# A row maximum that takes the factor as its scale, one bound operation for two heads, and bucket numbers turned by a small matmul, in hashed attention with a gated feed-forward behind it

## Chip, cores and metric

The kernel runs on one NeuronCore of a Trainium2 chip. The metric is device microseconds of one execution, from the first to the last instruction and what the runtime adds around it. Three runs of the kernel before gave 927.25, 927.81 and 928.17 us; the median is 927.81 us. The profile is of one more execution, of 924.44 us, in which the span of the instructions is 922.7 us.

## What is computed

The reference is attention in which a query sees only the keys of its own bucket, and then a feed-forward layer whose two inner products are multiplied with each other:

```python
q_bits = (np.einsum('bhsd,dk->bhsk', q, proj) > 0)      # batch 4, 8 heads, 768 rows, width 64; 6 bits
k_bits = (np.einsum('bhsd,dk->bhsk', k, proj) > 0)
mask = q_bucket[:, :, :, None] == k_bucket[:, :, None, :]   # bucket: the 6 bits as a number
scores = np.where(mask, q @ k.T / np.sqrt(64), -1e9)
attn = np.exp(scores - scores.max(-1)); attn /= attn.sum(-1) + 1e-09
x = (attn @ v), heads side by side                      # 3072 tokens x 512
out = ((x @ w_a) * (x @ w_b)) @ w_out                   # 512 -> 1536 -> 512
```

A query whose bucket holds no key gets equal weights, since all its scores are -1e9. Inputs and output are float32; the kernel splits nearly every operand into a high and a low float16 part and adds three matmul products for one.

## The kernel before

**Attention.** The 3072 tokens are taken in chunks of 128 or 256 (14 chunks; the first five are batch 0). Batch 0 has a path of its own (bits appended to the operands as extra rows, `qtile`). In batches 1 to 3 the work goes by pairs: 128 queries of two heads (72 pairs, so 144 tiles of 128 queries by 768 keys). A pair runs so:

- TensorE: 12 matmuls of the scores `s` for both heads into two PSUM buffers, of which there are only two (tag "s", L1286).
- VectorE: for each head the mask `hp` (L1333): -2^60 where the key's bucket number, held in all partitions as `trk[:, 1]`, differs from the query's. Then one custom operation (L1342) that writes e = scores + mask and the row maximum `mx`.
- VectorE: `bound`, two small operations for each head: `sc` (L1350), the factor cq = 1/8 times the scales of the q and k splits, or 0 where no key matched; and `bias` (L1354), 14 ln 2 - mx * sc, for which the constant `lnv` is held as a tile.
- ScalarE: exp(sc * e + bias) with the row sum (L1362).
- Split of e into two float16 parts `a`: the high part by ScalarE, VectorE or GpSimd (`cast`, L555), the low part by GpSimd or VectorE (`minus`, L558). A DMA transposes both into `at`, and 18 matmuls with v make `av` (L1263).

**Bucket numbers of the keys.** `split_pairs` makes, for each of the 12 head pairs of batches 1 to 3, a [128, 12] tile `bkk` of bucket numbers (row = key position within a block). They go to DRAM by one DMA, `buckets` (L852), come back broadcast to all partitions over the no longer needed raw keys `rk` (L857), and a copy on ScalarE or GpSimd (L555, out `trk`) puts them into the order by head and block.

**Feed-forward.** For each chunk `moe` issues 24 groups of `ab` matmuls (L1572; L1564 for the first two chunks, whose operands stay float32) into three PSUM buffers, ScalarE scales one product (`a`, L1593), VectorE multiplies it with the other (`g`, L1601), ScalarE and GpSimd split that into two float16 parts (L1612, L1617), and `o` matmuls (L1637) add them up. `osb` takes the result out.

**Order.** Every operation is recorded with `op`, and issued in the order of the table `ORDER`; `ENGINE_OF` says for operations that may run on two engines which one does. Each engine then runs its instructions in just that order, and waits at the head of its queue for what the next one needs. DMAs are issued from SyncE's queue, in order too.

Of the kernel before, what the change touches and what calls it, by code (L numbers as in the profile page):

```python
# [1747 lines left out]
```

## Time and profile before

| | |
|---|---|
| runs | 927.25, 927.81, 928.17 us |
| profiled execution | 924.44 us, span 922.7 us |
| TensorE matmul | 869.7 us busy (94%) |
| VectorE | 754.5 us (82%), 1839 instructions |
| ScalarE | 584.8 us (63%) |
| GpSimd | 380.9 us (41%) |
| TensorE's granted clock | full but for two short stretches, 0.996 in the mean |

The program is one long overlap: attention of later chunks beside the feed-forward of earlier ones. It begins with loads and the splitting of the first operands, and ends with some 90 us in which only the last feed-forward chunks are left. Matmul rows are pipelined and their ends are modelled, so TensorE's busy time also covers part of its short waits. An engine's waiting time is listed with the instruction that waited and with what ended the wait.

### The profile page before, as it was taken

What the parts mean: (1) busy time and instruction counts of PE and PEld (TensorE: products, weight loads), DVE (VectorE), ACT (ScalarE), POOL (GpSimd) and SP (SyncE); (2) the same over time, 40 slices, a digit from 0 to 9 for tenths busy, and PEclk for the clock granted to TensorE, in tenths of its full rate; (3) what the DMA queues carried; (4) which work ended last, traced back from release to release, by engine and by line L of the source; (5) the groups of instructions that cost most, each with busy time, mean ns of one, the idle gap of its engine ahead of it and who ended that gap; (6) DMA issues with size and microseconds to landing.
All of it is one profiled execution on the core that took longest, in us unless ns stands there. A gap on an engine that the chain in (4) does not pass through costs nothing. (4 is left out here: it accounts for less than half of the span.)

```text
span 922.7 us, 25179 instructions
## 1 busy us (share of the span) xinstructions
PE 869.7 (94%) x10049; PEld 653.4 (71%) x10049; DVE 754.5 (82%) x1839; ACT 584.8 (63%) x1130; POOL 380.9 (41%) x348
## 2 busy tenths in 40 slices
PE   5899999999999999999989999998999999999997
PEld 4788777677776666777666776766666777777775
DVE  7998999988879989868998889889879889974211
ACT  6878667566877677767556676565685665554222
POOL 1445546456465443442444442324433444432111
PEclk9999999999999999999999999999999999999999
DMA  9979997789889978988777877788877857776300
GB/s 328 299 246 262 163 166 147 127 162 194 162 166 163 178 133 138 162 172 181 147 150 121 133 139 126 143 161 159 151 152 146 140 113 125 116 126 98 48 35 24
DMA packets 396070, 140.69 MB, mean 152 GB/s; under 512 B 368176, under 2 KB 386736, under 8 KB 395952
## 3 DMA queue, kind: packets, MB, share of 16 engines
q1 hardware_dynamic: 395792, 139.08, 77.9%
q8 instruction: 78, 1.28, 0.6%
q14 instruction: 40, 0.33, 0.1%
q10 hardware_dynamic: 160, 0.00, 0.0%
HBM read 42.54 MB, written 6.33 MB: 53 GB/s over the span
## 5 line engine op out<-in xcount | busy, mean ns | idle before, releaser
L1572 PE MATMUL ab<-xT,wz 128*128 128x256 f16 (+1 forms) x3456 | 377.8, 264 | 14.3 <-DVE g L1601 9.7
L1572 PEld LDWEIGHTS <-wz 128*128 128x128 f16 x3456 | 308.6, 98 | 67.0 <-issue 26.4
L558 POOL TENSOR_TENSOR a<-e,a 128x768 f16<-128x768 f32 x123 | 207.6, 1691 | 141.5 <-ACT a L555 81.6
L1617 POOL TENSOR_TENSOR g<-g,g 128x256 f16<-128x256 f32 x132 | 96.9, 734 | 301.9 <-ACT g L1612 285.6
L1637 PE MATMUL o<-wz,g 128*128 128x512 f16 (+1 forms) x840 | 215.4, 392 | 1.2 <-DVE g L1601 0.6
L1362 ACT ACTIVATE e<-e,bias,sc 128x768 f32<-128x768 f32 x144 | 147.3, 1023 | 65.0 <-DVE bias L1354 64.7
L1342 DVE CUSTOM_DVE_ANT_0 e<-s,hp 128x768 f32<-128x768 f32 x144 | 136.1, 950 | 11.9 <-PE s L1286 7.3
L1263 PEld LDWEIGHTS <-at 128*128 128x128 f16 x3312 | 114.5, 98 | 31.9 <-DMA at<-a 12.3
L1593 ACT ACTIVATE a<-ab,ab 128x256 f32<-128x256 f32 x132 | 61.9, 469 | 115.6 <-PE ab L1572 109.6
L1601 DVE SCALAR_TENSOR_TENSOR g<-ab,ab,a 128x256 f32<-128x256 f32 x132 | 63.3, 479 | 83.7 <-ACT a L1593 71.3
L1263 PE MATMUL av<-vh,at 128*128 128x64 f16 x2208 | 121.0, 193 | 7.3 <-DMA at<-a 6.4
L1637 PEld LDWEIGHTS <-g 128*128 128x128 f16 x792 | 72.7, 98 | 72.3 <-issue 4.3
L1612 ACT CAST g<-g 128x256 f16<-128x256 f32 x132 | 52.9, 400 | 66.6 <-DVE g L1601 53.2
L555 ACT CAST a<-e 128x768 f16<-128x768 f32 x110 | 90.8, 827 | 5.1 <-DMA at<-a 3.0
L1286 PE MATMUL s<-trk,trq 64*128 64x384 f16 x864 | 86.5, 324 | 3.6 <-DVE mx L1342 2.9
L1354 DVE SCALAR_TENSOR_TENSOR bias<-mx,sc,lnv 128x1 f32<-128x1 f32 x144 | 73.2, 509 | 5.1
L1333 DVE TENSOR_SCALAR hp<-trk,bkq 128x768 bf16<-128x768 f16 x144 | 68.9, 492 | 3.0 <-ACT trk L555 2.0
L1286 PEld LDWEIGHTS <-trq 64*128 64x128 f16 x864 | 38.6, 94 | 39.0 <-issue 17.8
L558 DVE TENSOR_TENSOR a<-e,a 128x768 f16<-128x768 f32 x61 | 59.5, 977 | 5.9 <-ACT a L555 5.4
L1392 ACT ACTIVATE e<-s,bias,sc 128x768 f32<-128x768 f32 x48 | 47.4, 988 | 24.7 <-DVE bias L1383 13.5
L1263 PE MATMUL av<-vl,at 128*128 128x64 f16 x1104 | 62.4, 193 | 0.0
L1371 DVE TENSOR_REDUCE mx<-s 128x1 f32<-128x768 f32 x48 | 45.6, 950 | 4.8 <-PE s L1309 4.8
(206 smaller groups left out, 1063.7 us busy)
## 6 DMA issues: line engine op xcount, KB each, us to landing
rq<-in_q_dram SPq DMA_DIRECT2D x24, 256.0 KB, 3.7
rk<-in_k_dram SPq DMA_DIRECT2D x16, 384.0 KB, 4.3
wz<-in_moe_w_a_dram SPq DMA_DIRECT2D x12, 512.0 KB, 6.4
wz<-in_moe_w_b_dram SPq DMA_DIRECT2D x12, 512.0 KB, 5.0
...
```

Source lines behind the costliest of these rows:

```text
L555: {"ACT": nc.scalar.copy, "DVE": nc.vector.tensor_copy, "POOL": nc.gpsimd.tensor_copy}[e](out=out, in_=x)
L558: (nc.gpsimd if e == "POOL" else nc.vector).tensor_tensor(out=out, in0=x, in1=y, op=ALU.subtract)
L1263: nc.tensor.matmul(av.t[:, u, :], lhsT=at.t[:, a + kt, :], rhs=w.t[:, h, kt, :], start=i == 0, stop=i == 3 * NT - 1,)
L1286: nc.tensor.matmul(ps[h].t[:, jj, :HALF], lhsT=trq.t[rows, 0, qp * nq + j * nt + t], rhs=tr.t[rows, 0, k0 : k0 + NT // 2].rearrange("p n s ...
L1333: lambda: nc.vector.tensor_scalar(out=apart(), in0=tr.t[:, 1, h * NT : (h + 1) * NT].rearrange("p n s -> p (n s)"), scalar1=qbk[m, half].t ...
L1342: lambda: nc.vector.tensor_tensor_reduce(out=flat2(e.t), in0=halves(ps.t), in1=flat2(apart()), scale=1.0, scalar=-3.0e38, op0=ALU.add, op1 ...
L1354: nc.vector.scalar_tensor_tensor(out=bias.t[:, col], in0=mx.t[:, col], scalar=sc.t[:, col], in1=lnv, op0=ALU.mult, op1=ALU.subtract, rever ...
L1362: lambda: nc.scalar.activation(e.t, e.t, AF.Exp, bias=bias.t[:, col], scale=sc.t[:, col], accum_out=sm.t[:, u : u + 1]),
L1572: nc.tensor.matmul(pl.t[:, m, to], lhsT=wt(m, wi, cc, f), rhs=xt.t[:, cc * nt // NC, xi, cc * nt % NC : cc * nt % NC + nt, :], start=i == ...
L1601: lambda a=a, g32=g32, pl=pl, gr=gr, sc_of=sc_of: nc.vector.scalar_tensor_tensor(out=g32.t, in0=pl.t[:, 1, :CH], scalar=sc_of(gr + 1), in1 ...
L1617: lambda g=g, g32=g32, g_of=g_of: nc.gpsimd.tensor_tensor(out=g_of(g[1]), in0=g32.t, in1=g_of(g[0]), op=ALU.subtract),
L1637: nc.tensor.matmul(po[u].t.rearrange("p a b -> p (a b)"), lhsT=x()[:, us], rhs=w, start=f == 0 and i == 0, stop=f == NF - 1 and i == len(t ...
```

## The change

1. The custom maximum takes the factor cq as its `scale` operand in place of 1.0, so e = cq * scores + mask and `mx` is already scaled. `sc` goes; exp has no scale operand; a row in which no key matches keeps -2^60 in e and in `mx`, and the bias cancels it.
2. `bound` is one operation for both heads of a pair, [128, 2]: bias = 14 ln 2 - mx, and may run on VectorE or GpSimd. Both maxima come before it, and both exps after it. `lnv` goes.
3. The key buckets, now bfloat16, are turned by a matmul with the identity into PSUM (`kn`, 12 x 128), copied to SBUF by ScalarE or VectorE, written to DRAM as 12 rows of 256 bytes, and read back broadcast straight into `trk[:, 1]`. The copy out of `rk` goes. The blocks now lie as (block, head), so the mask reads every second block of 128.
4. `ORDER` and `ENGINE_OF` are new. Operations were renumbered; the engines' queues are the same up to about the first ninth of TensorE's.

```diff
-        line = nc.dram_tensor(f"buckets_{x}", [P, n], F16, kind="Internal").ap()
-        op(
-            "SP", DMA_ISSUE, lambda: nc.sync.dma_start(out=line, in_=bk.t), key, r=[bk], w=[("line", x)], svc=0.1,
-        )
-        over = lambda: raw.t.bitcast(F16)
+        pst = psum(f"{which}n_{x}", tag)
+        op("PE", 0.08, lambda: nc.tensor.matmul(pst.t[:n, 0, :P], lhsT=bk.t, rhs=identb, start=True, stop=True),
+           key, r=[bk, "identb"], w=[pst])
+        turned_bk = lambda: bits.t.bitcast(BF16)[:n, :P]
+        op(
+            "ACT DVE", {"ACT": 0.2, "DVE": 0.2}, lambda e: cast(e, turned_bk(), pst.t[:n, 0, :P]), key, r=[pst, bk],
+            w=[(bits, 2)],
+        )
+        line = nc.dram_tensor(f"buckets_{x}", [n, P], BF16, kind="Internal").ap()
+        op(
+            "SP", DMA_ISSUE, lambda: nc.sync.dma_start(out=line, in_=turned_bk()), key, r=[(bits, 2)],
+            w=[("line", x)], svc=0.1,
+        )
         op(
             "SP", DMA_ISSUE,
             lambda: nc.sync.dma_start(
-                out=over(), in_=line.rearrange("p n -> (p n)").unsqueeze(0).to_broadcast([P, P * n])
+                out=dst.t[:, 1].rearrange("p n s -> p (n s)").bitcast(BF16),
+                in_=line.rearrange("n p -> (n p)").unsqueeze(0).to_broadcast([P, P * n]),
             ),
-            key, r=[("line", x)], w=[raw], svc=1.3,
-        )
-        op(
-            "ACT POOL", {"ACT": 1.5, "POOL": 1.65},
-            lambda e: cast(
-                e, dst.t[:, 1].rearrange("p (h t) s -> p h t s", h=2), over().rearrange("p (s t h) -> p h t s", t=nb, h=2)
-            ),
-            key, r=[raw], w=[(dst, 1)], sbuf=True,
+            key, r=[("line", x)], w=[(dst, 1)], svc=1.3,
```

```diff
+    def pair_tile(m, half, j, t, st, key):
...
+        for h in range(2):
+            e = f3(f"e_{m}_{half}_{j}_{h}_{t}", ("e", NEXP))
...
+                lambda h=h, col=col, apart=apart: nc.vector.tensor_scalar(
+                    out=apart().rearrange("p (t s) -> p t s", t=NT),
+                    in0=tr.t[:, 1].rearrange("p (t h) s -> p t h s", h=2)[:, :, h].bitcast(BF16),
+                    scalar1=qbk[m, half].t[:, col], scalar2=-APART, op0=ALU.not_equal, op1=ALU.mult,
+                ),
+                key, r=[(tr, 1), qbk[m, half]], w=[(mask, h)], sbuf=True,
...
+                lambda e=e, h=h, col=col, apart=apart: nc.vector.tensor_tensor_reduce(
+                    out=flat2(e.t), in0=halves(ps[h].t), in1=flat2(apart()), scale=cq.t[:, j : j + 1],
+                    scalar=-3.0e38, op0=ALU.add, op1=ALU.max, accum_out=mx.t[:, col],
+                ),
+                key, r=[ps[h], (mask, h), (cq, j)], w=[e, (mx, u + h)],
...
+        def bound(eng):
+            ve = nc.gpsimd if eng == "POOL" else nc.vector
+            ve.tensor_scalar(
+                out=bias.t[:, cols], in0=mx.t[:, cols], scalar1=-1.0, scalar2=LN_ESC, op0=ALU.mult, op1=ALU.add
+            )
+
+        op(
+            "DVE POOL", {"DVE": 0.21, "POOL": 0.33}, bound, key, r=[(mx, u), (mx, u + 1)],
+            w=[(bias, u), (bias, u + 1)],
+        )
...
+                lambda e=e, col=col: nc.scalar.activation(
+                    e.t, e.t, AF.Exp, bias=bias.t[:, col], accum_out=sm.t[:, col]
+                ),
+                key, r=[(bias, u + h)], w=[e, (sm, u + h)],
...
-            def bound():
-                nc.vector.tensor_scalar(
-                    out=sc.t[:, col], in0=mx.t[:, col], scalar1=-APART / 2, scalar2=cq.t[:, j : j + 1],
-                    op0=ALU.is_gt, op1=ALU.mult,
-                )
-                nc.vector.scalar_tensor_tensor(
-                    out=bias.t[:, col], in0=mx.t[:, col], scalar=sc.t[:, col], in1=lnv, op0=ALU.mult,
-                    op1=ALU.subtract, reverse1=True,
-                )
-
-            op("DVE", 0.46, bound, key, r=[(mx, u), (cq, j), "pairs"], w=[(sc, u), (bias, u)])
```

Of the table of the order, its first changed line stands for the rest:

```diff
-    9, 219, 333, 702, 192, 193, 220, 347, 549, 213, 214, 269, 221, 252, 194, 711, 402, 404, 365, 321, 551, 550, 215,
+    219, 333, 702, 192, 193, 220, 347, 549, 213, 214, 269, 221, 252, 194, 711, 402, 404, 365, 321, 551, 550, 215, 108,
```

The new lists place 36 of the 72 bounds on VectorE and 36 on GpSimd. Beside that they move ten of the low parts of e from GpSimd to VectorE (61 and 123 before, 71 and 113 now), let VectorE make 66 high parts instead of 59 and seven of the 12 copies of turned buckets (ScalarE five), and give it four more of the q splits.

VectorE's queue, at the last pair of chunk 7 (`e`, `mx` and `bias` with the numbers of half, pair, head and block; `hp` the mask; `a` the high and low part of e; "ISA" is the custom maximum, its second row the read of its result), before:

```order
L1342 ISA e_1_1_1_1_7221,mx_1_6636<-s_1_1_1_1_7186,hp_80 128x768 [waits PE_49]
L1342 ISA mx_1_6636 128x1
L1350 TENSOR_SCALAR sc_1_6675<-mx_1_6636,cq_1_5880 128x1 [waits DVE_49]
L1354 SCALAR_TENSOR_TENSOR bias_1_6677<-mx_1_6636,sc_1_6675,lnv 128x1 [waits DVE_49]
L555 CAST a_7_1_1_1_1_7246<-e_1_1_1_1_7221 128x768 [waits DMAHW2_49,DMAHW1_49,Activation_49]
L1333 TENSOR_SCALAR hp_80<-trk_3_4351,bkq_1_6317 128x768
L1342 ISA e_1_1_0_1_7259,mx_1_6636<-s_1_1_1_0_7184,hp_80 128x768 [waits DVE_49]
L1342 ISA mx_1_6636 128x1
L1350 TENSOR_SCALAR sc_1_6675<-mx_1_6636,cq_1_5880 128x1 [waits DVE_49]
L1354 SCALAR_TENSOR_TENSOR bias_1_6677<-mx_1_6636,sc_1_6675,lnv 128x1 [waits DVE_49]
```

The same place now:

```order
L1317 ISA e_1_1_1_1_7159,mx_1_6567<-s_1_1_1_1_7135,hp_79,cq_1_5835 128x768 [waits PE_49]
L1317 ISA mx_1_6567 128x1
L1308 TENSOR_SCALAR hp_79<-trk_3_4299,bkq_1_6391 128x768
L1317 ISA e_1_1_0_1_7164,mx_1_6567<-s_1_1_1_0_7133,hp_79,cq_1_5835 128x768 [waits DVE_49]
L1317 ISA mx_1_6567 128x1
L1327 TENSOR_SCALAR bias_1_6667<-mx_1_6567 128x2 [waits DVE_49]
L556 CAST a_7_1_0_1_1_7236<-e_1_0_1_1_6705 128x768 [waits DMAHW1_49,Activation_49]
L559 TENSOR_TENSOR a_7_1_0_1_1_7236<-e_1_0_1_1_6705,a_7_1_0_1_1_7236 128x768 [waits DVE_49]
L1613 SCALAR_TENSOR_TENSOR g_4_7243<-ab_4_7167,ab_6_6584,a_4_7239 128x256 [waits Activation_49,Pool_49]
```

Four small operations between the two maxima and behind them are one, and the second maximum follows the first with only its mask between; the bias of both heads is ready only after the second.

GpSimd's queue about the first pair of chunk 8, whose bounds stood on VectorE (`g`: the low part of the feed-forward's product; `x`: the low part of the attention's output), before:

```order
L558 TENSOR_TENSOR x_7_0_7254<-x_0_7135,x_7_0_7254 128x512 [waits DMAHW3_49,Activation_49,Pool_49]
L558 TENSOR_TENSOR a_7_1_1_1_1_7246<-e_1_1_1_1_7221,a_7_1_1_1_1_7246 128x768 [waits DMAHW1_49,DVE_49]
L1617 TENSOR_TENSOR g_6_4_7454<-g_4_7291,g_6_4_7306 128x256 [waits Activation_49]
L1617 TENSOR_TENSOR g_6_5_7498<-g_5_7464,g_6_5_7466 128x256 [waits PE_49,Activation_49]
L1617 TENSOR_TENSOR g_6_6_7611<-g_6_7547,g_6_6_7609 128x256 [waits Activation_49]
L1617 TENSOR_TENSOR g_6_7_7632<-g_7_7626,g_6_7_7630 128x256 [waits Activation_49]
L558 TENSOR_TENSOR x_7_1_7670<-x_1_7647,x_7_1_7670 128x512 [waits DMAHW3_49,DVE_49,Activation_49]
```

The same stretch now:

```order
L1629 TENSOR_TENSOR g_6_3_7183<-g_3_7157,g_6_3_7181 128x256 [waits PE_49,Activation_49]
L559 TENSOR_TENSOR a_7_1_1_1_1_7245<-e_1_1_1_1_7159,a_7_1_1_1_1_7245 128x768 [waits DMAHW4_49,DMAHW5_49,DVE_49,Activation_49]
L559 TENSOR_TENSOR a_7_1_1_0_1_7271<-e_1_1_0_1_7164,a_7_1_1_0_1_7271 128x768 [waits DMAHW0_49,DVE_49,Pool_49]
L1629 TENSOR_TENSOR g_6_4_7311<-g_4_7243,g_6_4_7307 128x256 [waits PE_49,Activation_49]
L1327 TENSOR_SCALAR bias_0_7371<-mx_0_7335 128x2 [waits DVE_49]
L1629 TENSOR_TENSOR g_6_5_7404<-g_5_7373,g_6_5_7378 128x256 [waits PE_49,Activation_49]
L559 TENSOR_TENSOR a_8_0_0_1_0_7458<-e_0_0_1_0_7334,a_8_0_0_1_0_7458 128x768 [waits DMAHW3_49,Activation_49,Pool_49]
L1629 TENSOR_TENSOR g_6_6_7517<-g_6_7479,g_6_6_7494 128x256 [waits PE_49,Activation_49]
```

The bound `bias_0_7371` of chunk 8 stands behind low parts that wait for ScalarE, and in front of more of them.

## Rows read from the trace of the kernel before

**Rows 1.** The page, busy time, share of the span and instructions.

```profile
PE 869.7 (94%) x10049; PEld 653.4 (71%) x10049; DVE 754.5 (82%) x1839; ACT 584.8 (63%) x1130; POOL 380.9 (41%) x348
```

**Rows 2.** Windows: busy us (instructions) of PE, PEld, DVE, ACT, POOL; clock, DMA, GB/s.

```profile
0.00:92.00 92.00, 76.23 (x795) 66.37 (x796) 80.88 (x188) 70.74 (x105) 36.47 (x54) 0.98 0.96 284
92.00:828.00 736.00, 703.69 (x8457) 520.80 (x8455) 649.26 (x1600) 486.97 (x966) 325.72 (x270) 1.00 0.83 149
828.00:922.70 94.70, 89.80 (x805) 66.19 (x801) 24.33 (x53) 27.06 (x61) 18.76 (x25) 0.99 0.27 50
```

**Rows 3.** Waits of TensorE: us in total, times, longest.

```profile
PE ab L1572 <- DVE g L1601: 9.7, 13, 2.2
PE av L1263 <- DMA at<-a: 6.4, 8, 1.6
PE s L1286 <- DVE mx L1342: 2.9, 6, 0.9
```

**Rows 4.** The eleven 23 us windows with VectorE busiest, 92 to 828 us.

```profile
92.00:115.00 23.00, 22.59 (x253) 17.34 (x251) 21.80 (x59) 15.68 (x29) 12.60 (x11) 1.00 0.95 159
...
782.00:805.00 23.00, 22.90 (x300) 17.38 (x300) 21.74 (x53) 13.53 (x32) 9.43 (x8) 1.00 0.81 133
sum 253.00, PE 238.63 PEld 177.79 DVE 237.31 ACT 157.97 POOL 119.45; mean PE 21.69 PEld 16.16 DVE 21.57 ACT 14.36 POOL 10.86
```

**Rows 5.** The nine windows there with VectorE least busy.

```profile
207.00:230.00 23.00, 22.16 (x364) 17.87 (x362) 19.11 (x36) 15.68 (x30) 15.02 (x17) 1.00 1.04 189
...
805.00:828.00 23.00, 22.86 (x263) 16.99 (x262) 18.18 (x46) 11.79 (x24) 8.98 (x8) 1.00 0.77 127
sum 207.00, PE 201.10 PEld 150.40 DVE 166.10 ACT 145.44 POOL 94.63; mean PE 22.34 PEld 16.71 DVE 18.46 ACT 16.16 POOL 10.51
```

**Rows 6.** Groups by line and form: busy us, mean ns, idle before.

```profile
L1354 DVE SCALAR_TENSOR_TENSOR bias<-mx,sc,lnv 128x1 f32<-128x1 f32 x144 | 73.2, 509 | 5.1
L1350 DVE TENSOR_SCALAR sc<-mx,cq 128x1 f32<-128x1 f32 x144 | 29.9, 208 | 1.9
L1342 DVE CUSTOM_DVE_ANT_0 e<-s,hp 128x768 f32<-128x768 f32 x144 | 136.1, 950 | 11.9 <-PE s L1286 7.3 <-issue 0.9 <-DVE hp L1333 0.9
L558 POOL TENSOR_TENSOR a<-e,a 128x768 f16<-128x768 f32 x123 | 207.6, 1691 | 141.5 <-ACT a L555 81.6 <-DVE a L555 34.1 <-PE o L1637 7.1
L558 DVE TENSOR_TENSOR a<-e,a 128x768 f16<-128x768 f32 x61 | 59.5, 977 | 5.9 <-ACT a L555 5.4 <-issue 0.2
L555 DVE CAST a<-e 128x768 f16<-128x768 f32 x59 | 36.3, 615 | 6.4 <-ACT e L1362 6.4
L564 DVE TENSOR_SCALAR qt<-rq,ai_q 128x256 f16<-128x256 f32 x16 | 6.6, 454 | 0.2
L555 ACT COPY trk<-rk 128x1536 f16<-128x1536 f16 x7 | 20.8, 2970 | 0.5 <-DMA rk<-buckets 0.5
L831 ACT COPY neg_q<-qb 128x48 f32<-128x48 f32 x18 | 3.4, 188 | 6.7 <-PE qb L819 6.7
```

**Rows 7.** Timeline of 340.3 to 342.5 us: start, us, instruction.

```profile
340.48 1.64 POOL L558 TENSOR_TENSOR a<-e,a 128x768 f16<-128x768 f32 x1 [0.50 <-DVE a L555]
340.56 1.58 DVE L1354 SCALAR_TENSOR_TENSOR bias<-mx,sc,lnv 128x1 f32<-128x1 f32 x1
```

**Rows 8.** Single lines: count, ns min/median/max.

```profile
L1354 DVE SCALAR_TENSOR_TENSOR bias<-mx,sc,lnv x144: 219/221/1694, 228.0 to 844.3; 128x1 f32<-128x1 f32 x144
L1333 DVE TENSOR_SCALAR hp<-trk,bkq x144: 368/414/1878, 206.8 to 832.0; 128x768 bf16<-128x768 f16 x144
L1379 POOL TENSOR_SCALAR sc<-mx,cq x12: 297/298/1330, 29.6 to 216.1; 128x1 f32<-128x1 f32 x12
```

**Rows 9.** Waits of GpSimd and ScalarE: us, times, longest.

```profile
POOL g L1617 <- ACT g L1612: 285.6, 102, 6.5
ACT e L1362 <- DVE bias L1354: 64.7, 43, 4.4
```

More of the change, by code (lines that the diff above doesn't have):

```diff
@@ L617, in attention_moe @@
     two_to = cp.tile([P, NBITS], F32, tag="two_to", name="two_to")
-    lnv = cp.tile([P, 1], F32, tag="lnv", name="lnv")
     def pair_consts():
@@ L623, in pair_consts @@
         nc.gpsimd.memset(pjl, 0.0)
-        nc.gpsimd.memset(lnv, LN_ESC)
         for i in range(NBITS):
@@ L836, in split_pairs @@
         )
-        bk = buf(f"bk{which}", [P, n], F16 if side == 0 else F32, f"bk{which}_{x}", 2)
+        bk = buf(f"bk{which}", [P, n], BF16 if side == 0 else F32, f"bk{which}_{x}", 2)
         def bucket():
@@ L1269, in turn_and_sum @@
         op("PE", 0.53, outs, key, r=[at, vh, vl], w=[(av, u)])
-    def pair_scores(m, half, j, t, key):
+    def pair_tile(m, half, j, t, st, key):
         b, _, nt = CHUNKS[m]
@@ L1293, in pair_scores @@
         mask = Buf(plan, p2, "hp", NPREP, [P, 2 * S], F16, f"mask_{n}", None, ring)
-        return ps, mask
-    def qtile(m, half, j, h, t, st, key, pair=None):
+        bias, sm, cq = (st[x] for x in ("bias", "sm", "cq"))
+        mx = st["mx"]
+        u = (j * nt + t) * 2
+        if t == 0:
+            factor(m, half, j, b, hp, cq, key)
+        es = []
+        for h in range(2):
+            e = f3(f"e_{m}_{half}_{j}_{h}_{t}", ("e", NEXP))
+            es.append(e)
+            col = slice(u + h, u + h + 1)
+            apart = lambda h=h: mask.t[:, h * S : (h + 1) * S].bitcast(BF16)
+            op(
+                "DVE", 0.36,
+                lambda h=h, col=col, apart=apart: nc.vector.tensor_scalar(
[6 more added lines that the diff above has]
+            op(
+                "DVE", 1.04,
+                lambda e=e, h=h, col=col, apart=apart: nc.vector.tensor_tensor_reduce(
[4 more added lines that the diff above has]
+            )
@@ new lines, in pair_tile @@
+        cols = slice(u, u + 2)
+        def bound(eng):
[3 more added lines that the diff above has]
+            )
+        op(
+            "DVE POOL", {"DVE": 0.21, "POOL": 0.33}, bound, key, r=[(mx, u), (mx, u + 1)],
+            w=[(bias, u), (bias, u + 1)],
+        )
+        for h in range(2):
+            e = es[h]
+            col = slice(u + h, u + h + 1)
+            op(
+                "ACT", 1.04,
+                lambda e=e, col=col: nc.scalar.activation(
+                    e.t, e.t, AF.Exp, bias=bias.t[:, col], accum_out=sm.t[:, col]
+                ),
+                key, r=[(bias, u + h)], w=[e, (sm, u + h)],
+            )
+            turn_and_sum(e, f"{m}_{half}_{j}_{h}_{t}", b, hp, h, u + h, st, key)
@@ L1297, in qtile, with factor @@
+    def factor(m, half, j, b, hp, cq, key):
+        op(
+            "DVE", 0.16,
+            lambda: nc.vector.tensor_scalar(
+                out=cq.t[:, j : j + 1], in0=inv_of(qinv[m, half]), scalar1=inv_of(kinv[b, hp]), scalar2=0.125,
+                op0=ALU.mult, op1=ALU.mult,
+            ),
+            key - 1, r=[qinv[m, half], kinv[b, hp]], w=[(cq, j)],
+        )
+    def qtile(m, half, j, h, t, st, key):
         b, _, nt = CHUNKS[m]
@@ L1301, in qtile @@
         trq, tr = trqs[m, half], trk[b, hp]
-        ps = pair[0][h] if pair else psum(f"s_{n}")
+        ps = psum(f"s_{n}")
         def scores():
@@ L1313, in scores @@
                     )
-        if not pair:
-            op("PE", 0.65, scores, key, w=[ps], r=[(trq, 0), (trq, 1), (tr, 0), (tr, 1)])
+        op("PE", 0.65, scores, key, w=[ps], r=[(trq, 0), (trq, 1), (tr, 0), (tr, 1)])
         mx, bias, sc, sm, av, cq = (st[x] for x in ("mx", "bias", "sc", "sm", "av", "cq"))
         if h == 0 and t == 0:
-            op(
-                "DVE", 0.16,
-                lambda: nc.vector.tensor_scalar(
-                    out=cq.t[:, j : j + 1], in0=inv_of(qinv[m, half]), scalar1=inv_of(kinv[b, hp]), scalar2=0.125,
-                    op0=ALU.mult, op1=ALU.mult,
-                ),
-                key - 1, r=[qinv[m, half], kinv[b, hp]], w=[(cq, j)],
-            )
@@ L1369, in qtile @@
+            factor(m, half, j, b, hp, cq, key)
+        col = slice(u, u + 1)
         op(
@@ L1689, in attention_moe @@
                     for t in range(nt):
-                        pair = pair_scores(m, half, j, t, start + u)
-                        for h in range(2):
-                            qtile(m, half, j, h, t, st, start + u, pair)
-                            u += 1
+                        pair_tile(m, half, j, t, st, start + u)
+                        u += 2
                     continue
```

29 lines of the change are left out of this document (removed), and 409 rows, old and new, of tables (ENGINE_OF, ORDER).

## The prediction, made before the changed kernel ran

> **What bounds the kernel now.** I read the page's shares first, then the windows by stage, then TensorE's waits, and last the groups by line on the engine that TensorE waits for. The shares [rows 1] show TensorE's matmuls busy for 94% of the span and VectorE for 82%, with the others far below. The windows [rows 2] say where TensorE stands still: 92.00 - 76.23 = 15.8 us in the first 92 us, where operands load; 736.00 - 703.69 = 32.3 us between 92 and 828 us; 4.9 us at the end, where only the last result is taken out. So 32.3 us is what a change of the attention part can win from idle time that the profile shows; short waits under modelled matmul ends may add to it. The waits [rows 3] show who is late: mostly `g` of the feed-forward and the maximum, both on VectorE, and the transposes, which wait for the split of e. In the same stretch VectorE is busy for 649.26 of 736 us, 88%. It runs in order, so a `g` behind two maxima of 0.95 us each is late although VectorE has idle time elsewhere. Both engines are near their end, TensorE nearer.
>
> How strongly does TensorE's idle time hang on VectorE's load? I cut 92 to 828 us into 32 windows of 23 us. In the eleven with VectorE busy for at least 21.0 us, the means are 21.57 us for VectorE and 21.69 for TensorE [rows 4]; in the nine with VectorE below 19.7 us they are 18.46 and 22.34 [rows 5]. So 3.11 us less VectorE work goes with 0.65 us more TensorE work, 0.209 us for one. That is no law, since the windows also hold different work, but it is the only price for VectorE's load that this trace gives.
>
> **The change, part by part.** *The bound.* 144 `bias` at 0.509 us (73.2 us) and 144 `sc` at 0.208 us (29.9 us) leave VectorE [rows 6]: 103.1 us. In their place come 36 bounds on VectorE and 36 on GpSimd. The trace has no operation of this shape. From below it is `sc`, an operation with one source, 0.208 us; from above `bias` with its waits, 0.509 us. That gives 7.5 to 18.3 us for VectorE's 36; I take 7.5, since `sc` is the nearer row. On GpSimd the nearest is the `sc` of batch 0, 0.298 us in the median and 1.33 at worst [rows 8]: 11 to 48 us on an engine that is busy 41%; its work is covered, its place in the queue is the slow rival below.
>
> *Work put on VectorE by the new lists.* Ten low parts at 0.977 us, seven high parts at 0.615, four q splits at 0.454 [rows 6] and seven copies of turned buckets, for which the nearest row is ScalarE's `neg` at 0.188 [rows 6]: 9.8 + 4.3 + 1.8 + 1.3 = 17.2 us. Two `sc` and two `bias` of batch 0 go to GpSimd, 0.8 us at the price of `sc`. VectorE's sum: -103.1 + 7.5 + 17.2 - 0.8 = -79 us; with the dear bound -68 us.
>
> *The maximum with an operand as scale.* The element stream is the same, 0.950 us [rows 6]; I take no change. Below it there is nothing to win, as it reads and writes what it did. From above, the slowest elementwise operation on 768 elements is GpSimd's 1.691 us [rows 6]: 144 x 0.741 = +107 us.
>
> *The mask on every second block.* 0.414 us in the median now [rows 8]. The rows of 128 stay contiguous and the element size stays two bytes, so I take no change; if the blocks cost it its rate, VectorE's own full-rate operation on 768 elements, 0.977 us, is the upper end: 144 x (0.977 - 0.414) = +81 us. Less than 0.368, the shortest of them, would be a surprise; that end is worth -7 us.
>
> *Turned buckets.* Twelve copies of some 2.97 us [rows 6] leave ScalarE (seven) and GpSimd (five), which TensorE does not wait for, so the time itself is worth nothing; the raw buffer comes free earlier and the chain to a pair's first mask is shorter by the copy and longer by a matmul, a small copy and two hops. TensorE gets 12 matmuls. The mean of all of its matmuls is 869.7 / 10049 = 0.087 us [rows 1], so 1 us, and that is on the path. They borrow a PSUM buffer for a moment, and the bucket's DMA now also waits for a copy on ScalarE or VectorE; behind it on SyncE's queue stand the transposes `at`. Both are covered as long as that copy is not queued behind long work. Without cover I price each of the 12 at TensorE's mean wait for a transpose, 6.4 / 8 = 0.8 us [rows 3]: up to +10 us; I take 0.
>
> *Order of the pair.* The first head's exp now waits for the second mask and maximum too, about 1.4 us more. ScalarE has room for that, and what it waits for here today, 64.7 us in 43 waits on `bias` [rows 9], costs TensorE nothing that its rows show. The new order is otherwise the same work interleaved anew.
>
> *Sum.* -79 us at 0.209 is -16.5 us for TensorE's idle time, plus 1 us of matmuls: -15.5 us. The profiled execution of 924.44 us becomes 908.9; it lies 3.4 us under the median of the runs, so I expect 912.3 us. With the dear bound (-68 us): 914.6.
>
> **A rule that speaks against it.** The rows first: `bias` takes 0.221 us in the median and 1.694 at most [rows 8], and one of the long ones begins at 340.56 us, 0.08 us after a subtract on GpSimd, and ends 0.02 us after it [rows 7]. So 73.2 - 144 x 0.221 = 41.4 us of what `bias` cost was no work but a wait for GpSimd. The mask, too, has a maximum of 1.878 against its median of 0.414 [rows 8].
>
> The Trainium skill, "SBUF — State Buffer", section "Who interferes with whom", says that VectorE and GpSimd share one port pair and that a VectorE operation with two SBUF inputs, or one in a two-port mode, is fully blocked while GpSimd holds it. The trace agrees, with the 1.58 us of [rows 7]. By that page the new bound, with two elements of one source, may be blocked too, where `sc` with one element was not; this is the dear bound above.
>
> From the rows alone follows a rival: GpSimd's subtracts stay, so the wait need not vanish with `bias`; the next operation that shares with GpSimd (mask, cast, subtract) can meet it instead.
>
> **The rivals.**
> 1. *The wait moves on.* VectorE is relieved of 79 - 41.4 = 38 us only: 38 x 0.209 = 7.9, plus 1: -6.9 us, so 920.9 us. For it: the subtracts still run for 113 x 1.691 = 191 us. Against: `bias` came right behind the maximum, just when GpSimd works on another e, and 0.6 of the time GpSimd does nothing.
> 2. *All idle time goes.* VectorE at (649 - 79) / 736 = 77% lets the planner keep TensorE fed: -32.3 + 1, so 896.5 us. Against: part of the waits is for transposes, whose number stays, with the DMA engines busy at 0.83 [rows 2].
> 3. *Hidden anyway.* The nine lighter windows hold lighter work rather than a freer VectorE, or the mask loses its rate (+81 us on VectorE eats the -79): 927 us.
> 4. *Slower: bounds stuck on GpSimd.* GpSimd waits 285.6 us in 102 waits, 2.8 us each, for ScalarE's part of `g` [rows 9], and the new lists put 36 bounds into that queue between just those low parts. A bound caught there holds two exps, their e buffers (four in all, two pairs) and then the next maxima and scores. Each one that reaches TensorE costs 2.8 us, so from six on (15.5 / 2.8) the win is gone; with ten, 912.3 + 28 = 940 us. Against: bounds wait now as well, ScalarE up to 4.4 us, without TensorE showing it. A maximum at GpSimd's rate would end there too: (107 - 79) x 0.209 + 1 = +7 us, 935 us.
>
> **How the numbers follow.** My forecast has 0.52, rival 1 0.15, rival 2 0.08, rival 3 0.08, rival 4 0.17. Under 0.2% of 927.81 us, 1.9 us, is what a measurement of this kernel can hardly tell from no change. The forecast, rivals 1 and 2 are faster: 0.75. Rival 3 is mostly no change: 0.08. Rival 4 is slower: 0.17. The forecast's own range is 904 to 918 us, from a slope half as steep again to the dear bound with a few turned buckets uncovered. To hold the time 8 times in 10 the range reaches down to near rival 2 and up into rival 4: 899 to 934 us. The time is 912 us.
>
> **What would show it.** No `sc` and `bias` groups on VectorE in batches 1 to 3, its busy time at 675 us (rival 1: some 717); the mask still at 0.41 us in the median, the maximum at 0.95. TensorE's idle time between 92 us and the end of attention at some 16 us, with `ab` waiting less for `g`. Rival 1 shows in a mask or cast whose mean moves away from its median. Rival 4 shows in exps that wait for a bound on GpSimd and in scores that wait for maxima. I am wrong in the mechanism if VectorE is lighter by 60 us or more and TensorE's idle time stays.

## The result and the profile after

The changed kernel takes 892.38 us (median of 4 runs, 891.94 to 894.51), the kernel before beside it 927.99 us: a ratio of 0.9618, 95% interval 0.9597 to 0.9639. That is 35.6 us less, where 15.5 had been forecast, and below the range of 899 to 934 us. The profiled execution took 891.99 us.

The page, as [rows 1]:

```profile
span 890.2 us, 24962 instructions
PE 863.4 (97%) x10061; PEld 650.9 (73%) x10061; DVE 696.0 (78%) x1608; ACT 550.2 (62%) x1122; POOL 369.9 (42%) x370
```

The windows, with the columns of [rows 2]:

```profile
0.00:92.00 92.00, 78.43 (x815) 67.92 (x816) 81.00 (x190) 72.90 (x109) 37.75 (x40) 0.98 0.99 289
92.00:828.00 736.00, 726.71 (x8810) 540.54 (x8808) 603.88 (x1393) 462.93 (x982) 321.76 (x316) 1.00 0.84 153
828.00:890.20 62.20, 58.21 (x445) 42.40 (x441) 11.15 (x26) 14.34 (x33) 10.41 (x15) 1.00 0.08 24
```

TensorE now stands idle for 736.00 - 726.71 = 9.3 us in the middle stretch; it was 32.3 [rows 2]. Over the whole span its idle time fell from 53.0 to 26.8 us (-26.2), and its busy time by 6.3 us, though it has 12 matmuls more. Together they are the 32.5 us by which the span is shorter. Of the 6.3 us, the granted clock (0.998 in the mean against 0.996) explains at most 0.002 x 866 = 1.7; the rest I put down to short waits hidden under modelled matmul ends, which no row shows by itself. VectorE is down by 58.5 us, not by 79.

TensorE's waits, the lines that answer to [rows 3], and GpSimd's and ScalarE's for and behind the bound:

```profile
PE ab L1584 <- DVE g L1613: 3.3, 5, 1.1
PE av L1264 <- DMA at<-a: 3.0, 4, 1.8
...
POOL bias L1327 <- DVE mx L1317: 28.9, 16, 8.7
...
ACT e L1340 <- POOL bias L1327: 11.4, 11, 2.4
```

The waits for `g` fell from 9.7 to 3.3 us, those for transposes from 6.4 to 3.0, and those of scores for a maximum are gone. GpSimd stands behind maxima for 28.9 us at its bounds, but no wait of TensorE names a bound.

Groups by line and form, as [rows 6], and single lines (ns min/median/max), as [rows 8]:

```profile
L1317 DVE CUSTOM_DVE_ANT_0 e<-s,hp,cq 128x768 f32<-128x768 f32 x144 | 143.5, 1011 | 23.7 <-PE s L1287 19.7 <-POOL a L559 0.6 <-DVE hp L1308 0.3
L1340 ACT ACTIVATE e<-e,bias 128x768 f32<-128x768 f32 x144 | 133.8, 929 | 26.1 <-DVE bias L1327 14.4 <-POOL bias L1327 11.4
L559 DVE TENSOR_TENSOR a<-e,a 128x768 f16<-128x768 f32 x71 | 70.5, 995 | 3.7 <-ACT a L556 3.3
L556 DVE CAST a<-e 128x768 f16<-128x768 f32 x66 | 42.4, 644 | 6.5 <-ACT e L1340 3.9 <-DMA at<-a 1.6 <-DMA trq<-qt 0.8
...
L1327 DVE TENSOR_SCALAR bias<-mx x36: 156/170/1579, 214.4 to 811.4; 128x2 f32<-128x2 f32 x36
L1327 POOL TENSOR_SCALAR bias<-mx x36: 192/193/894, 245.2 to 787.8; 128x2 f32<-128x2 f32 x36
...
L1308 DVE TENSOR_SCALAR hp<-trk,bkq x144: 369/413/1885, 210.3 to 797.7; 128x768 bf16<-128x768 bf16 x144
```

The maximum with an operand as scale takes 1011 ns against 950 [rows 6]; the mask kept its median (413 against 414 [rows 8]). VectorE's bound has a median of 170 ns but a maximum of 1579. Fourteen of the 36 take over 300 ns, and in the trace each of them ends within 80 ns of the end of an operation on GpSimd; the longest (start, us, instruction):

```profile
374.99 1.64 POOL L559 TENSOR_TENSOR a<-e,a 128x768 f16<-128x768 f32 x1
375.08 1.58 DVE L1327 TENSOR_SCALAR bias<-mx 128x2 f32<-128x2 f32 x1
```

### The profile page after: what moved, and what is told of

It reads as the page before. It is cut to its first block, busy times and chain, and to the rows that moved or that the text cites. A ratio compares the mean times of both kernels' runs of the same rounds, so it can differ in the third digit from the quotient of the medians.

```text
span 890.2 us, 24962 instructions
## 1 busy us (share of the span) xinstructions
PE 863.4 (97%) x10061; PEld 650.9 (73%) x10061; DVE 696.0 (78%) x1608; ACT 550.2 (62%) x1122; POOL 369.9 (42%) x370
## 4 chain that ended last, share of the span: by engine, by line
PE 74%; DVE 12%; DMA 7%; issue 3%; ACT 2%; POOL 1%; SPq 0%; DVEq 0%; ACTq 0%; POOLq 0%
PE ab L1584 34%; PE o L1649 18%; PE av L1264 9%; PE s L1287 7%; DMA at<-a 4%; PE ab L1576 2%; PE s L1370 2%; DVE mx L1383 2%; DVE wz L1009 1%; DVE e L1317 1%; DMA wz<-in_moe_w_a_dram 1%; DVE g L1613 1%; ACT e L1404 1%; DMA wz<-in_moe_w_out_dram 1%; DVE a L556 1%
## 5 line engine op out<-in xcount | busy, mean ns | idle before, releaser
L559 POOL TENSOR_TENSOR a<-e,a 128x768 f16<-128x768 f32 x113 | 194.1, 1723 | 137.1 <-ACT a L556 65.1
L1629 POOL TENSOR_TENSOR g<-g,g 128x256 f16<-128x256 f32 x132 | 101.6, 769 | 275.4 <-ACT g L1624 256.7
L1317 DVE CUSTOM_DVE_ANT_0 e<-s,hp,cq 128x768 f32<-128x768 f32 x144 | 143.5, 1011 | 23.7 <-PE s L1287 19.7
L1340 ACT ACTIVATE e<-e,bias 128x768 f32<-128x768 f32 x144 | 133.8, 929 | 26.1 <-DVE bias L1327 14.4
L556 ACT CAST a<-e 128x768 f16<-128x768 f32 x106 | 87.0, 827 | 4.1 <-DMA at<-a 2.6
L1287 PE MATMUL s<-trk,trq 64*128 64x384 f16 x864 | 83.0, 324 | 0.0
L1308 DVE TENSOR_SCALAR hp<-trk,bkq 128x768 bf16<-128x768 bf16 x144 | 74.6, 528 | 0.2
L559 DVE TENSOR_TENSOR a<-e,a 128x768 f16<-128x768 f32 x71 | 70.5, 995 | 3.7 <-ACT a L556 3.3
L1576 PE MATMUL ab<-xT,wz 128*128 128x128 f32 x384 | 49.2, 278 | 0.0
```

The costliest lines, as they stand in the source:

```text
L556: {"ACT": nc.scalar.copy, "DVE": nc.vector.tensor_copy, "POOL": nc.gpsimd.tensor_copy}[e](out=out, in_=x)
L559: (nc.gpsimd if e == "POOL" else nc.vector).tensor_tensor(out=out, in0=x, in1=y, op=ALU.subtract)
L1287: nc.tensor.matmul(ps[h].t[:, jj, :HALF], lhsT=trq.t[rows, 0, qp * nq + j * nt + t], rhs=tr.t[rows, 0, k0 : k0 + NT // 2].rearrange("p n s ...
L1308: lambda h=h, col=col, apart=apart: nc.vector.tensor_scalar(out=apart().rearrange("p (t s) -> p t s", t=NT), in0=tr.t[:, 1].rearrange("p ( ...
L1317: lambda e=e, h=h, col=col, apart=apart: nc.vector.tensor_tensor_reduce(out=flat2(e.t), in0=halves(ps[h].t), in1=flat2(apart()), scale=cq. ...
L1340: lambda e=e, col=col: nc.scalar.activation(e.t, e.t, AF.Exp, bias=bias.t[:, col], accum_out=sm.t[:, col]),
```

## The experiments

All times are medians, beside runs of the kernel before on the same chip (927.1 to 927.3 us; 928.0 beside the changed kernel). The intervals are some 2 us to either side, so a difference of 3 us between two rows is at the edge of what they can tell, and a price that rests on 3 to 5 us is known to about half of itself. "VectorE" is its busy time, in which an operation that is blocked counts as busy; "wait for g" is TensorE's wait at `ab` for VectorE's `g`, in us.

| run | VectorE us | time us | ratio, 95% interval | wait for g |
|---|---|---|---|---|
| before | 754.5 | 927.3 | 1 | 9.7 |
| e1 one-source bias | 719.2 | 908.2 | 0.9792 [0.9769, 0.9815] | 1.8 |
| e2 bounds and maximum alone | 694.4 | 903.1 | 0.9739 [0.9719, 0.9758] | 1.1 |
| e11 = e2 + 2 idle | 731.3 | 908.4 | 0.9800 [0.9776, 0.9824] | 2.0 |
| e13 = e2 + 3 idle | 769.6 | 930.4 | 1.0052 [1.0030, 1.0073] | 9.2 |
| e14 = e2 without copies | 687.0 | 895.9 | 0.9670 [0.9645, 0.9695] | 0.4 |
| after | 696.0 | 892.4 | 0.9618 [0.9597, 0.9639] | 3.3 |
| e4 = after + 1 idle | 716.3 | 895.8 | 0.9657 [0.9639, 0.9676] | 3.7 |
| e10 = after + 2 idle | 741.9 | 908.6 | 0.9796 [0.9768, 0.9824] | 6.7 |
| e3 = after + 1 idle + 1 that waits | 765.8 | 925.6 | 0.9981 [0.9966, 0.9996] | 11.4 |
| e5 = after + 3 idle | 771.5 | 930.7 | 1.0051 [1.0032, 1.0071] | 18.1 |
| e7 one-column bounds | 689.7 | 892.3 | 0.9623 [0.9603, 0.9643] | 3.2 |
| e8 all bounds on VectorE, late | 698.6 | 899.5 | 0.9696 [0.9671, 0.9721] | 4.5 |
| e12 all bounds on VectorE, at once | 702.5 | 893.9 | 0.9644 [0.9615, 0.9673] | 3.2 |
| e6 copies ahead of the broadcast | 697.6 | 934.3 | 1.0081 [1.0058, 1.0103] | 2.6 |
| e9 copies beside the chain | 700.3 | 923.4 | 0.9962 [0.9937, 0.9988] | 14.0 |
| e15 small pieces on ScalarE | 695.2 | 895.6 | 0.9664 [0.9635, 0.9693] | 1.7 |

### What the load of VectorE costs

**e1**: the kernel before, its `bias` as an operation with one source (it leaves out the constant 14 ln 2).

```diff
-                nc.vector.scalar_tensor_tensor(out=bias.t[:, col], in0=mx.t[:, col], scalar=sc.t[:, col], in1=lnv, ...
+                nc.vector.tensor_scalar(out=bias.t[:, col], in0=mx.t[:, col], scalar1=sc.t[:, col], scalar2=-1.0, ...
```

> The kernel before, its order and its number of instructions unchanged; only the bias of a pair's tile has one tensor source (-mx * sc) in place of two, so that it need not wait for GpSimd. It leaves out the constant 14 ln 2 in the exponent. In the trace of before 144 x 0.221 = 31.8 of the 73.2 us of bias were work and 41.4 us a wait. Theory L (VectorE's load sets the time at the rate that the change showed, 32.5 us of span for 58.5 us of VectorE, 0.56): up to -23 us, 905 us, with bias at 0.21 us. Theory O (load is worth the 0.2 of the prediction, the rest came from the new order): -8 us, 920 us. Theory M (the wait moves on to the next operation that shares with GpSimd): bias short, mask and subtract longer, 926 to 928 us.

**e2**: the kernel before, in its order (two `cq` pulled forward), with the scaled maximum and one bound for each head.

```diff
-                    out=flat2(e.t), in0=halves(ps.t), in1=flat2(apart()), scale=1.0, scalar=-3.0e38, op0=ALU.add,
+                    out=flat2(e.t), in0=halves(ps.t), in1=flat2(apart()), scale=cq.t[:, j : j + 1], scalar=-3.0e38, op0=ALU.add,
...
+                    out=bias.t[:, col], in0=mx.t[:, col], scalar1=-1.0, scalar2=LN_ESC, op0=ALU.mult, op1=ALU.add
...
-                    e.t, e.t, AF.Exp, bias=bias.t[:, col], scale=sc.t[:, col], accum_out=sm.t[:, u : u + 1]
+                    e.t, e.t, AF.Exp, bias=bias.t[:, col], accum_out=sm.t[:, u : u + 1]
```

> The kernel before in its own order (two cq are pulled forward by a place or two), with the scaled maximum and one bound operation for each head on VectorE in place of sc and bias; no pairing of bounds, no turned buckets, no new lists. VectorE: -103.1 us for sc and bias, +30 for 144 bounds at 0.208, +8.8 for the maximum, which takes 1.011 us in place of 0.950 in the changed kernel: -64 us. Theory L: -36 us, 892 us, all of the gain without the new order. Theory O: 64 x 0.2 = -13 us, 915 us, and the other 20 us belong to the new lists. If both count, between.

**e3, e4**: the changed kernel, with results that nobody reads written behind each maximum: in e4 an operation like the old `sc`, in e3 that and one like the old two-source `bias`.

```diff
+                    nc.vector.tensor_scalar(out=sc.t[:, col], in0=mx.t[:, col], scalar1=-APART / 2, ...   # e3, e4
+                    nc.vector.scalar_tensor_tensor(out=sc.t[:, col], in0=mx.t[:, col], scalar=sc.t[:, col], in1=lnv, ...   # e3
```

> The changed kernel in its new order, with two idle operations behind each of the 144 maxima on VectorE whose results nobody reads: one like the old sc, one like the old bias with its two tensor sources. +62 us of work on VectorE, up to +103 with waits for GpSimd as before. Theory L: +35 to +58 us, 927 to 950 us, the whole gain gone. Theory O: +13 to +21 us, 905 to 914 us, since the new lists keep their part.

> The changed kernel in its new order, with only the one idle operation like the old sc behind each maximum (one tensor source, one element, no wait for GpSimd): +30 us on VectorE. Theory L: +17 us, 909 us. Theory O: +6 us, 898 us. Together with the run that puts both back it gives the price of VectorE's load at two points.

Groups of e1, and of e3 (the operation put back):

```profile
L1354 DVE TENSOR_SCALAR bias<-mx,sc 128x1 f32<-128x1 f32 x144 | 30.8, 214 | 5.1
```

```profile
L1329 DVE SCALAR_TENSOR_TENSOR sc<-mx,sc,lnv 128x1 f32<-128x1 f32 x144 | 62.8, 436 | 5.0
```

In e1 `bias` falls from 73.2 us [rows 6] to 30.8 at the same count: with one source it does not wait for GpSimd. That took 19.1 us off the time for 35.3 us of VectorE, 0.54 for one; e1 to e2 gave 5.1 for 24.8 us, 0.21, and the changed kernel to e4 3.4 for 20.3, 0.17. No single price fits all of it: mine of 0.209 fits the last two, and the 0.56 that the change as a whole showed (32.5 us of span for 58.5 of VectorE) fits e1. In e2 the exps also lose their scale operand, 13 us of ScalarE's time; at what e15 paid for 35 us there (3.2 us, below) that is worth about 1 us, an estimate. Two readings were left: a wait for GpSimd is dearer than work, or any time on VectorE is dearer the more there already is.

**e5, e10, e11, e13** add only idle one-source operations, which do not wait: three and two behind each maximum of the changed kernel, two and three ahead of each bound of e2.

```diff
+                for _ in range(2):   # 3 in e13; the same operation behind the maximum in e10 and e5
+                    nc.vector.tensor_scalar(out=sc.t[:, col], in0=mx.t[:, col], scalar1=-APART / 2, scalar2=cq.t[:, j : j + 1], ...
```

> The changed kernel with three idle one-source operations behind each scaled maximum (432 more operations of one element a row on VectorE, results unread), so that VectorE carries as much time as in the run with the two operations put back (765.8 us) or more, but none of it waits for GpSimd. e4 measured 20.3 us more VectorE time for 144 of them, e3 a mean of 214 ns: 61 to 92 us here, VectorE busy 757 to 788 us. Theory W (work costs 0.17 to 0.2 us per us, only a wait for GpSimd costs more): 903 to 911 us. Theory C (each further us of VectorE costs more than the one before, whatever it is): 922 us or more, as e3.

> The changed kernel with two idle one-source operations behind each scaled maximum, between e4 (one: 716.3 us of VectorE, 895.8 us) and e5 (three: 771.5 us, 930.7 us): VectorE busy some 744 us. Theory C (the price of a us of VectorE rises with the load): 904 to 912 us. A straight line from the changed kernel to e5 (0.51 us per us): 917 us. A step between two and three: 898 us or 926 us.

> e2 (the old order, 694.4 us of VectorE, 903.1 us) with two idle one-source operations ahead of each bound: VectorE busy some 742 us, nothing of the added time waits for GpSimd. Theory C, by the old order's own points e1 (719.2 us, 908.2 us) and before (754.5 us, 927.3 us): 916 to 922 us. Theory W (waits for GpSimd are what made before slow, work costs 0.2 us per us): 911 to 914 us.

> The old order as in e11, with three idle one-source operations ahead of each bound in place of two. e11 had 731.3 us of VectorE and 908.4 us; two operations there added 36.9 us, so one more gives some 750 us, close to the 754.5 us of the kernel before, but with no bound that waits for GpSimd. Theory C (what counts is VectorE's time in all, work or wait, and beyond some 730 us each further us costs 0.5 or more, as from e10 to e5): 918 to 926 us. Theory W (in the old order the waits for GpSimd were dearer than work): 909 to 913 us.

The idle operations in e13, and what TensorE waits for in e5:

```profile
L1365 DVE TENSOR_SCALAR sc<-mx,cq 128x1 f32<-128x1 f32 x432 | 91.3, 212 | 12.0
```

```profile
PE ab L1599 <- DVE g L1628: 18.1, 24, 2.6
```

With added operations that do not wait for GpSimd, both orders climb back to the time of before. e5 and e10 came out as the theory of the load (C) said; e11, at 908.4 us, lay below both of its ranges, and e13, at 930.4, above both, with 769.6 us of VectorE where some 750 had been expected. In the changed order one us more of VectorE costs 0.17 us up to 716 us, (908.6 - 895.8) / 25.6 = 0.50 up to 742, and 22.1 / 29.6 = 0.75 up to 772. In the old order it is 5.3 / 36.9 = 0.14 up to 731 and 22.0 / 38.3 = 0.57 up to 770. So the price depends on the load. And e3, with 62.8 - 144 x 0.221 [rows 8] = 31 us of waiting in it, took 925.6 us at 765.8 us of VectorE, where the straight line from e10 to e5 has 926.4: time in which VectorE is blocked costs the same as time in which it works. The theory of the dearer wait falls for the changed order. In the old one e13 speaks against it as well, but the kernel before lies at 927.3, 5.6 us above the line from e11 to e13 at 754.5 us (921.7). Of that some 1.5 us is what e1, with its slower exp, lies above the line from e2 to e11 too; the rest stays open, and a dearer wait is not excluded there.

All the added operations stand between a maximum and its bound, so they lengthen each pair's chain as well as VectorE's load, and no run puts them elsewhere. TensorE's waits speak for the load: in e5 they name `g` of the feed-forward, with 18.1 us, far more than the maxima or the transposes of the pairs:

```profile
PE av L1265 <- DMA at<-a: 4.2, 4, 2.3
...
PE s L1288 <- DVE mx L1319: 1.7, 5, 0.8
```

**e7**: VectorE's 36 bounds as two operations of one column.

```diff
-            ve.tensor_scalar(out=bias.t[:, cols], in0=mx.t[:, cols], ...
+            for cs in [cols] if eng == "POOL" else [slice(u, u + 1), slice(u + 1, u + 2)]:
+                ve.tensor_scalar(out=bias.t[:, cs], in0=mx.t[:, cs], ...
```

> The changed kernel with VectorE's 36 bounds of two columns as two operations of one column each (GpSimd's 36 stay). The two-column one has a median of 0.167 and a mean of 0.430 us, so 9.5 us of 15.5 are wait; one-column ones took 0.148 in e2, so 72 cost 10.7 us. Theory W (0.5 to 0.8 us per us of wait, 0.17 to 0.2 per us of work): 885 to 889 us. Theory C (the same rate for both, some 0.2 on a net of -4.8 us): 891 to 892 us. If one-column ones wait as well here: 893 to 896 us.

The line of e7, as [rows 8]:

```profile
L1328 DVE TENSOR_SCALAR bias<-mx x72: 135/148/155, 213.6 to 812.2; 128x1 f32<-128x1 f32 x72
```

The wait is gone, 155 ns at most against 1579 with two columns, VectorE is 6.3 us lighter, and the time is the same within the 2 us or so of the intervals. Less load on VectorE hardly helps the changed kernel any more; at 0.17 the 6.3 us would be worth 1.1 us, which these runs cannot tell from nothing.

### Copies and turned buckets

**e14**: e2 without the 12 copies; the broadcast goes straight to where the mask reads, and the kernel leaves out the rearranging.

```diff
-        over = lambda: raw.t.bitcast(F16)
+        over = lambda: dst.t[:, 1].rearrange("p n s -> p (n s)")
...
-            lambda e: cast(e, dst.t[:, 1].rearrange(...), over().rearrange(...)),
+            lambda e: None,
```

> e2 (the old order, 903.1 us) without the 12 copies that rearrange the bucket numbers: the broadcast goes straight into the place that the mask reads, in the order in which the numbers stand, so that the rearranging is left out of the computation. Some 35.8 us leave ScalarE and GpSimd, and the chain to a pair's first mask is a copy shorter. Theory T (the copies were part of what the old order paid, as they were dear in e6 and e9): 893 to 899 us. Theory N (the old order had its place for them; the new lists gain by their order): 901 to 904 us.

903.1 became 895.9 us, so the copies cost the old order 7.3 us. VectorE lost 7.4 us of busy time by it at the same number of operations, worth 1.0 at 0.14; the rest, by subtraction, is what the copies did to ScalarE, GpSimd and the chain. TensorE's listed waits fall from 33.7 to 26.2 us in small amounts: for maxima, results on their way out and transposes 1.4 to 2.9 us each, for `g` only 0.7.

**e6, e9**: copies of the same size in the changed kernel, in e6 directly ahead of the broadcast, in e9 with the transpose at the head of the chain (in the kernel before they were 7 on ScalarE and 5 on GpSimd). **e15**: the same time on ScalarE in 144 small pieces.

```diff
+            (nc.scalar.copy if on_act else nc.gpsimd.tensor_copy)(out=..., in_=...)   # e6, e9: [128, 1536], 8 on ScalarE, 4 on GpSimd
+                    nc.scalar.copy(out=flat2(e.t)[:, 0, :64], in_=flat2(e.t)[:, 0, :64]),   # e15, behind each exp
```

> The changed kernel with a copy of the bucket numbers back in the chain ahead of each broadcast that had one (8 on ScalarE, 4 on GpSimd); its result is overwritten by the broadcast. Theory T (the turned buckets, which need no copy, are what gains the 10.7 us between e2 and the changed kernel): 898 to 903 us, with TensorE's waits in the chains. Theory N (the new lists and the pairing gain it, the copies lay beside other work): 891 to 895 us.

> As e6, but the 12 copies are issued with the transpose at the head of the chain instead of directly ahead of the broadcast (source and result are other data, overwritten by the broadcast), so that SyncE's queue finds them done. ScalarE and GpSimd carry the same 35 us. Theory Q (e6 lost its 42 us since the broadcast stood at the head of SyncE's queue for 55 us and held up the transposes behind it): 891 to 896 us. Theory A (the time on ScalarE and GpSimd itself is dear): 910 us or more.

> The changed kernel with one small copy in place (64 elements a row) on ScalarE behind each of the 144 exps, some 0.25 us each, 36 us in all: as much as the 12 copies of e9, but in small pieces. Theory B (e9 lost 31 us since a block of 3 us that the lists have no place for makes g late by as much): 893 to 900 us. Theory A (any time on ScalarE is as dear, 0.87 us per us): 915 us or more.

SyncE's queue (SPq) and TensorE in e6, as [rows 3]:

```profile
SPq L871 <- POOL trk L867: 20.8, 3, 11.1
SPq L871 <- ACT g L1631: 20.5, 4, 8.7
SPq L871 <- ACT trk L867: 14.0, 3, 9.0
...
PE av L1271 <- DMA at<-a: 21.9, 8, 9.5
```

In e6 the broadcast (L871) stood at the head of SyncE's queue for 55 us until ScalarE or GpSimd were done with its copy, and the transposes behind it came late. Its time, 934.3 us, is beyond both expectations. I held the queue for the cause; e9 shows that it is not all of it, for there no broadcast waits for a copy and 31 of the 42 us are lost even so. Its timeline about the longest gap (start, us, instruction; idle before):

```profile
433.44 2.98 ACT L811 COPY trk<-kt 128x1536 f16<-128x1536 f16 x1
436.32 0.93 ACT L563 ACTIVATE kt<-rk,ai_k 128x768 f16<-128x768 f32 x1
...
437.29 1.15 DVE L798 SCALAR_TENSOR_TENSOR kt<-rk,ai_k,kt 128x384 f16<-128x384 f32 x2 [4.48 <-ACT kt L563]
...
438.57 2.88 POOL L811 COPY trk<-kt 128x1536 f16<-128x1536 f16 x1 [3.26 <-DVE cq L1359]
...
441.42 0.67 POOL L1638 TENSOR_TENSOR g<-g,g 128x256 f16<-128x256 f32 x1
...
442.12 0.48 DVE L1622 SCALAR_TENSOR_TENSOR g<-ab,ab,a 128x256 f32<-128x256 f32 x1 [2.96 <-POOL g L1638]
...
442.65 4.92 PE L1593 MATMUL ab<-xT,wz 128*128 128x256 f16 x24 [4.78 <-DVE g L1622]
...
498.59 2.79 PE L1593 MATMUL ab<-xT,wz 128*128 128x256 f16 x24
```

And windows of e9 before, in and behind that gap:

```profile
432.00:437.00 5.00, 5.00 (x68) 3.99 (x67) 0.81 (x2) 4.97 (x5) 1.65 (x1) 1.00 1.16 168
437.80:442.60 4.80, 0.07 (x4) 0.00 (x1) 1.84 (x6) 0.95 (x2) 4.03 (x3) 0.75 0.87 170
442.65:447.60 4.95, 4.95 (x27) 3.53 (x27) 3.21 (x7) 1.88 (x6) 2.37 (x2) 0.55 0.34 117
```

Two copies follow each other here. The one on ScalarE stands before the high part of `kt`, for which VectorE waits 4.48 us to make the low part; the copy on GpSimd reads that low part, so it stands at the head of its queue for 3.26 us and then runs for 2.88. Behind it stands the low part of `g`, whose buffer VectorE's next `g` needs, whose result TensorE needs: a gap of 4.78 us. Of the four copies on GpSimd this is the only one that had to wait. Behind the gap the granted clock was 0.55, close to the lower level of 1.2 GHz, and 24 `ab` matmuls took 4.92 us, where 24 later ones at full clock took 2.79.

A copy on GpSimd can also block VectorE. Two of the four did, by the trace; this one lies at the second longest of the gaps that wait for `g`:

```profile
384.79 2.91 POOL L811 COPY trk<-kt 128x1536 f16<-128x1536 f16 x1
385.02 2.69 DVE L1561 SCALAR_TENSOR_TENSOR back<-x_mx,back 128x1 f32<-128x1 f32 x1
...
388.28 0.96 PE L1593 MATMUL ab<-xT,wz 128*128 128x256 f16 x7 [2.77 <-DVE g L1622]
```

In the whole profiled execution of e9, whose span is 35.1 us longer than the changed kernel's, TensorE is idle for 49.0 us instead of 26.8 and busy for 12.9 us more, at a mean clock of 0.983 against 0.998. Eight of its gaps of more than 1 us, 18.8 us together, begin between the start of a copy and 1.5 us after its end. Between 300 and 700 us the granted clock falls below 0.9 behind six gaps; in the changed kernel it does not fall there. So about half of the loss is gaps at copies and about a third the lower clock.

The 35 us of e15, in pieces of 244 ns, cost 3.2 us:

```profile
L1342 ACT COPY e<-e 128x64 f32<-128x64 f32 x144 | 35.2, 244 | 4.5
```

So it is not time on ScalarE as such that is dear but a block of 3 us at a place for which the lists had not been made. The place counts, for in the old order, whose lists had the 12 copies, they cost 7.3 us. Blocks on GpSimd were not tried in small pieces, so the share of the four there, two of which block VectorE, is not separated.

### Bounds on GpSimd

**e8, e12**: all bounds on VectorE, one column each, in e8 where the lists have them, in e12 directly behind each maximum.

```diff
-            ve = nc.gpsimd if eng == "POOL" else nc.vector
+            for cs in [slice(u, u + 1), slice(u + 1, u + 2)]: nc.vector.tensor_scalar(...)   # e8; in e12 inside the maximum's step
```

> As e7, and GpSimd's 36 bounds are done on VectorE too, at the places where the lists have them for GpSimd, 144 one-column operations in all. Some 10.7 us more of VectorE; GpSimd loses 11.4 us of work and 28.9 us of waiting for VectorE's maximum, so its subtractions start earlier. Theory W (work alone counts, GpSimd's waits lie beside other work): 887 to 891 us, 2 over e7. Theory G (GpSimd's waits for the maximum delay the sums that TensorE waits for): under e7, 880 to 885 us.

> The changed kernel with each head's bound as a one-column operation on VectorE directly behind that head's maximum, none on GpSimd. VectorE as in e8 (698.6 us). Theory P (e8 lost 7 us since its bounds stood at the places of the lists for GpSimd, too late on VectorE, and exp waited 47 us for them): 890 to 894 us. Theory G (the bounds on GpSimd are what gains, since exp need not wait behind VectorE's queue): 897 to 901 us.

ScalarE's waits for these bounds, of e8 and of e12:

```profile
ACT e L1340 <- DVE bias L1327: 47.4, 33, 5.9
```

```profile
ACT e L1342 <- DVE bias L1322: 5.9, 8, 1.4
```

With the late ones the exps wait for 47.4 us, and the time is 7 us over e7, above both ranges expected for e8; at once they wait for 5.9 us, and the time is 893.9, as theory P said. The 1.5 us to 892.4 lie within the intervals, so a gain from the hand-over to GpSimd is not shown.

## Why the prediction was wrong

Divided by the experiments: -19.1 us for the wait of `bias` (e1), -5.1 for the scaled maximum and what goes with it (e2), -7.3 for the copies (e14), and -3.5 for all else (new lists, pairing, GpSimd's bounds, and what the turning itself costs), 35 us in all. I had -16.5 for VectorE's load and +1 for the turned buckets. At my price the 60.1 us of e1 and e2 would bring 12.6 us, and they brought 24.2; the copies I put at nothing. These two steps, 11.6 and 7.3 us, make nearly all of the 19.5 us that were missing.

- **The price of VectorE's load: the failed step.** That VectorE's load holds up TensorE was right; its price was not. The slope of 0.209 from window classes [rows 4, 5] was called "the only price for VectorE's load that this trace gives". Between runs 60.1 us less of VectorE (e2) brought 24.2 us, 0.40 for one, and e1 alone 0.54; over all runs the price goes from 0.14 to 0.75, in either order the higher the more loaded VectorE is. My own reading that VectorE was 88% busy in the middle stretch should have warned me of one slope. The windows carried little: over all 32 the slope is 0.15 with a correlation of -0.25, so the two classes that I compared hardly show a price at all. Why is only argued: a backlog that arises in one window is paid in later ones.
- **The load itself.** -79 us forecast, -58.5 measured; VectorE ended at 696, not 675. The bound took 15.5 us instead of 7.5 (36 at a mean of 430 ns, with waits for GpSimd: the dear bound); the maximum, "I take no change", took 7.4 us more; the mask's mean rose from 492 to 528 ns, 5 us; casts and low parts took 3 us over their estimate. At a flat 0.209 this error would have cost me 4 us; it went the other way, since the price was too low.
- **Copies and turned buckets: the second failed step.** "The time itself is worth nothing": wrong, 7.3 us. That no TensorE wait names a copy does not make it free: in e14 the waits that go are those for other work, and in e9 TensorE waits by name for `g`, which stands behind a copy.
- **TensorE's idle time.** I expected it at some 16 us in the middle stretch; it is 9.3, and TensorE's busy time fell by 6.3 us besides, for which I had no term.
- **Rivals.** Nearest came the second, *all idle time goes*, 896.5 us, to which I gave 0.08. Its number is near by luck: not all idle time went (23.0 of the 32.3 us did), the rest of the gain came from the two ends and the fall in busy time, and VectorE stands at 603.88 / 736 = 82% there, not 77%. Its reason, that a lighter VectorE lets TensorE be fed, fits e7, where 6.3 us less gain nothing that can be measured. The first, *the wait moves on*, has a small part: in e1 the mask's mean rose from 492 to 527 ns, 5 of the 42 us. The fourth did not come: exps do wait for GpSimd's bounds, 11.4 us, but no TensorE wait names a bound, and e12 without GpSimd's bounds is no faster.
- **The rule.** The bound of two columns waits, up to 1579 ns, and with one column not, up to 155 (e7). The Trainium skill, "SBUF — State Buffer", section "Who interferes with whom", puts it so: a VectorE operation with at most one SBUF input contends with GpSimd only in a two-port mode, which a `tensor_scalar`, as this bound is, can enter. The runs agree for two columns, and e1 with what it says of two inputs; that one column stays clear is what e7 shows.
